# Linear attention and a gated causal convolution on one core: tokens of q in sequence, every load on GpSimd's queue, and new tables of order

## The chip, the core and the metric

The kernel runs on one NeuronCore of one Trainium2 chip. The core has five engines with instruction streams of their own: PE (TensorE, matrix products and transposes), DVE (VectorE), ACT (ScalarE), POOL (GpSimd) and SP (SyncE, which here only issues transfers). They meet through semaphores. Sixteen DMA engines move data between the chip's memory and the core's SBUF. [...] PE writes to PSUM, eight banks of 128 partitions by 2 KB.

The metric is the device time of one execution in microseconds, the median of several runs. Lower is better. The kernel before took 217.03 us (three runs, 216.33 to 217.27).

## The reference

The inputs q, k, v have the shape (batch 8, heads 8, tokens 576, 64), float32. The features have 128 + 128 columns.

```python
def phi(x):
    proj = np.einsum('bhsd,df->bhsf', x, w_phi)
    proj = proj - np.max(np.abs(proj), axis=-1, keepdims=True)
    return np.concatenate([np.exp(proj), np.exp(-proj)], axis=-1)
q_p, k_p = (phi(q), phi(k))
kv = np.einsum('bhsf,bhsd->bhfd', k_p, v)
z = np.sum(k_p, axis=2)
num = np.einsum('bhsf,bhfd->bhsd', q_p, kv)
den = np.einsum('bhsf,bhf->bhs', q_p, z)[..., None] + 1e-06
x = num / den                        # then (b, s, heads * 64)
gate_pre = sum over k of conv_w[k] * x shifted by 4 - k tokens     # causal, 5 taps
gate = 1.0 / (1.0 + np.exp(-gate_pre))
out = gate * (x @ w_val) @ w_out     # (8, 576, 512) float32
```

## The kernel before

**The stages of one batch.** The eight batches run through the same stages, several batches in flight. A batch has 36 groups of 128 rows of k and as many of q; they are worked in five units, `UNITS` (four of 4 columns of 128, one of 2).

- *Load and transpose.* k and q are brought to SBUF with rows on the partitions and must be transposed to `kT` and `qT` (the 64 features of a row on the partitions, two rows side by side). Batch 0 is loaded as float32 by SP (`load32`, L521 to 527), transposed by PE in float32 (`tp32`, L536) and copied to bfloat16 by ACT or DVE (`tc32`, L542 and L544). Batch 1 is loaded as bfloat16 by POOL (`load`, L550) and transposed by PE (`tp16`, L555, copied at L560). From batch 2 on POOL loads to `KQN` and SP issues one DMA transpose for k and one for q (`xpose`, L565). Two small POOL copies (`hold`, `holdx`, L509 and L512) hold POOL's next loads back until earlier data have landed. v comes from SP (`loadv`, L531) but for batch 1.
- *The k side.* `kp` (PE, L577) projects; `kmax` (DVE, L585) takes maxima of the absolute values; `kexp` (ACT, L595) makes e^x and e^-x to `KTIL`; `ek` (ACT, L604) makes the scale of each row; `vs` (POOL, L610 and L611) scales v to `VT`; `st` (PE, L620) sums over tokens to the 65 columns of kv and z; `kv` copies them to bfloat16.
- *The q side.* `qm` and `qmax` (L577, L585), `mqt` and `mqr` (L658 to 670, the maxima transposed and negated), `rx` (POOL, L682: the maxima spread over an identity, so that a product with ones subtracts them), `qp` (PE, L693 and L698), `qexp` (ACT, L706 to `QTIL`, and for the last unit L709 to `QTT`).
- *Quotient and transpose back.* `num` (PE, L719, five chunks; the fifth is L726), `nrm` (DVE, L737 the reciprocal, L740 the product), `xtp` (PE, L748 and L752, or for batches 6 and 7 a DMA transpose by SP, `xtd`, L755) and `xtc`, which copies to `XT`, x with its 512 columns on the partitions. `halo` (POOL, L768 and L769) fills the tokens to the left of each half.
- *The MLP.* `gate` (PE, L781, the convolution as products with diagonal matrices), `tanh` (ACT, L785; the sigmoid is made from it), `val` (PE, L791), `gv` (DVE, L797), `gvc` (POOL, L805, collects the last 64 tokens of two batches), `out` (PE, L813 and L817), `oev` (the copy from PSUM, L630 or L634) and `odma` (the store by SP, 256 KB in rows of 2 KB, L830 and L836).

**Order of the tokens.** q of a batch is loaded as 128 equal contiguous rows of 9 KB (`rows`, L518), 16 partitions to a head. So a column of `qT` holds tokens 36 apart, the chunks of `num` hold every second row pair, and a chunk is not a stretch of the sequence: `XT` has two halves of 144 pairs of tokens, and `halo` copies what the causal shift needs from one place of this order to another. `num` of any chunk waits for all of `qexp` of its batch.

**Order of the work.** Nothing is scheduled on the chip or at build time. `build` lists about a thousand tasks; `ORDER` gives the order in which they are issued (each engine takes its own in that order), `FLEX` which of two or three engines takes a task that can go to several, and `BANKS` the PSUM banks. `WARM` puts in products of ones (6 here, L491), `ZERO` adds products with zeros to a PSUM bank in use (150 here, L497 and L504) at places in the first quarter of the order. An engine waits at an instruction until its data are there, and all behind it on that engine wait too.

Of the kernel before, what the change touches and what calls it, by code (L numbers as in the profile page):

```python
# [17 lines left out]
F = 128  # L18
DM = 512
# [5 lines left out]
NU = len(UNITS)  # L25
PEB = 1
QPART = ((0, 1), (2, 3, 4))
XB = (6, 7)
HOLDU = 4
NO = 8  # L30
NJ = 2 * NC
XH = R // 2
HALO = 16
XW = HALO + XH
WARM = (
    "60:6:1 81:1:1 87:7:2 134:7:1 141:7:1 "
)
ZERO = "35:76:7 61:80:5 75:34:1 101:105:1 126:215:8 144:223:1 155:192:4 158:200:1 175:315:6 189:346:1 195:241:2 197:241:2 211:327:1"
STD = 1.18
E1 = D + 1  # L40
QW = 2 * NR

ORDER = (
# [36 lines left out]
)  # L80
FLEX = (
    "AAAAAADAAADDPPPPDDDDAADDDDDDDDDDDDDAAADAAAADDDDAAADDDAADAAADDADAADDDDADDDDADDDDDDAADADDAAAAAA"
)
BANKS = (
    "037362307001454523232323016701676714232367230101676012354423010145454501013660564675601456745010145450101676767014501454"
    "545672012376701230167676745677773567232367232345452301672323232367674545015452343623670101232345454452230145450167676767"
    "010123014501230167450120167364012345236745454555723014545234567232323010123236745230167232346701422010167454567010121656"
    "701456701012301670123010167232367674567023677260123230123230167464644501016701670123676745672345232345450123670157672345"
    "010167452326322345670145670101674545012345012367452345010127452301014545670101765"
# [3 lines left out]
class Task:  # L93

    __slots__ = ("kind", "b", "u", "engs", "durs", "fn", "deps", "grp", "also", "opens", "mode", "eng", "lat", "idx", "wait", "rank")
# [5 lines left out]


def out_seq(b, c):
    return 9 * (b // 2) + (4 * (b % 2) + c)


LAT = {"PE": 0.17, "ACT": 0.17, "DVE": 0.17, "POOL": 0.2, "SP": 0.7, "DMA": 1.3}
MSW = 0.05


def dve(n, ov=0.075):
    return n / 960.0 + ov


def act(n):
    return n * 0.000833 + 0.067


class Plan:
# [9 lines left out]
    def add(self, kind, b, u, eng, dur, fn=None, deps=(), grp=None, mode=0, lat=None, also=None, wait=0.0, rank=None):  # L129
        t = Task()  # L130
        t.kind, t.b, t.u, t.fn = kind, b, u, fn
        t.engs = (eng,) if isinstance(eng, str) else eng
        t.durs = (dur,) if isinstance(eng, str) else dur
        t.deps = [d for d in deps if d is not None]
        t.grp, t.also, t.mode, t.lat, t.wait, t.rank = grp, also, mode, lat, wait, rank
        t.opens = []
        for g in (grp, also):
            if g is not None:
                if g.left == 0:
                    t.opens.append(g)  # L140
                g.left += 1
        t.eng = t.engs[0]
        t.idx = len(self.tasks)
        self.tasks.append(t)
        return t

    def follow(self):

        names = {"A": "ACT", "D": "DVE", "P": "POOL"}
# [13 lines left out]
def build(plan, em=None):  # L163
# [11 lines left out]
    def G(*k):  # L175
        return h.get(k)
# [724 lines left out]
```

## Time and profile before

One profiled execution has a span of 215.4 us from the first to the last instruction; the runs' median of 217.03 us includes the start and end around it.

| | us | share of the span |
|---|---|---|
| span of the profiled execution | 215.4 | |
| median of the runs | 217.03 | |
| ACT: `kexp` and `qexp` (L595, L706, L709) | 71.8 + 62.5 + 10.0 | 67% |
| ACT: all | 180.6 | 84% |
| DVE: the two maxima (L585) | 44.3 + 43.6 | 41% |
| POOL: all, of it `vs` (L610) | 132.9, 67.9 | 62%, 32% |
| mean busy share of the 16 DMA engines, the queue of SP and ACT | | 56.8% |
| the same, POOL's queue | | 26.2% |

A row of a group reads: line, engine, operation, output tile and input tile with their shapes, count, then the busy time of all and the mean of one in ns, then the idle time ahead of them and who ended it. The mean of one is longer than busy time over count where instructions overlap. In a view of stretches each engine has its busy time and, in brackets, its instructions; PEclk is the clock that the throttle granted (1.00 is full). In a timeline a row reads start, duration, engine, line, what, and how many are merged. "SPq" and "POOLq" rows of DMA issues are the issue; the time to landing stands in the view of transfers.

### The profile page before, as it was taken

The numbers are of one execution on the slowest core, as the hardware profiler recorded it, in microseconds if no ns is written. First come the engines' busy times: TensorE is split into PE (matmuls) and PEld (weight loads), VectorE is DVE, ScalarE is ACT, GpSimd is POOL, SyncE is SP. The second block draws the span as 40 slices with busy tenths as digits, with TensorE's granted clock in tenths as the row PEclk, the third lists the DMA queues.
The fourth block names the chain that finished last, engine by engine and source line by source line (L and its number), as shares of the span: only waits on it lengthen the run. The fifth ranks groups of instructions, "written<-read, shape, count | busy, mean of one in ns | idle before, by whom it ended". The sixth has DMA issues, their size and how long they took to land.

```text
span 215.4 us, 9005 instructions
## 1 busy us (share of the span) xinstructions
PE 194.6 (90%) x3924; PEld 138.9 (64%) x3944; DVE 170.2 (79%) x257; ACT 180.6 (84%) x267; POOL 132.9 (62%) x172
## 2 busy tenths in 40 slices
PE   2887978778999999989999999999999999899990
PEld 2665566566766767667767677568757766687640
DVE  3299999999699978998899978998699897654510
ACT  3699999999999899998899997999988988634251
POOL 3045999996984649952997099903992879210010
PEclk9999999999999999999999999999999999999998
DMA  6999979999799699979997878979962264864166
GB/s 180 381 226 208 291 162 159 277 198 199 139 165 286 118 153 250 290 130 200 237 279 134 96 165 251 188 151 173 287 211 84 67 161 126 83 168 99 49 188 205
DMA packets 49954, 39.92 MB, mean 185 GB/s; under 512 B 34165, under 2 KB 39541, under 8 KB 49914
## 3 DMA queue, kind: packets, MB, share of 16 engines
q1 hardware_dynamic: 43616, 28.65, 56.8%
q0 software_dynamic: 6032, 10.49, 26.2%
q8 instruction: 31, 0.51, 1.0%
q10 hardware_dynamic: 266, 0.21, 0.3%
q14 instruction: 9, 0.07, 0.1%
HBM read 30.48 MB, written 9.44 MB: 185 GB/s over the span
## 4 chain that ended last, share of the span: by engine, by line
PE 55%; ACT 18%; DVE 15%; issue 4%; DMA 4%; SPq 0%; DVEq 0%; ACTq 0%
PE PS L791 12%; PE PS L781 9%; PE PS L813 9%; ACT QTIL L706 7%; ACT KTIL L595 7%; DVE MQP L585 6%; PE PS L719 5%; PE PS L577 5%; PE PS L620 4%; DVE MK L585 2%; PE PS L693 2%; DMA KTIL<-in_k_dram 2%; DMA XT<-XN 2%; PE PS L536 2%; DVE XN L740 2%
## 5 line engine op out<-in xcount | busy, mean ns | idle before, releaser
L595 ACT ACTIVATE KTIL<-PS 128x1024 bf16<-128x1024 f32 (+1 forms) x80 | 71.8, 965 | 3.5 <-PE PS L577 1.7
L610 POOL TENSOR_TENSOR VT<-VN,EK 128x1152 bf16<-128x1152 f32 x32 | 67.9, 2123 | 2.9 <-ACT EK L604 2.8
L706 ACT ACTIVATE QTIL<-PS 128x1024 bf16<-128x1024 f32 x64 | 62.5, 1051 | 1.9 <-PE PS L698 1.4
L682 POOL TENSOR_TENSOR RX<-MQR,ident 128x512 bf16<-128x512 bf16 (+1 forms) x39 | 36.6, 963 | 36.2 <-DVE MQR L670 32.8
L585 DVE TENSOR_REDUCE MK<-PS 128x8 f32<-128x1024 f32 (+1 forms) x40 | 44.3, 1113 | 2.9 <-PE PS L577 1.2
L585 DVE TENSOR_REDUCE MQP<-PS 128x8 bf16<-128x1024 f32 (+1 forms) x40 | 43.6, 1112 | 2.1 <-PE PS L577 1.2
L791 PE MATMUL PS<-XT,WV 128*128 128x288 bf16 x256 | 34.8, 286 | 0.3 <-DVE GV L797 0.2
L797 DVE SCALAR_TENSOR_TENSOR GV<-TH,PS 128x576 bf16<-128x576 bf16 x32 | 23.8, 752 | 10.4 <-PE PS L791 4.7
L813 PE MATMUL PS<-WOUT,GV 128*128 128x512 bf16 x110 | 29.7, 380 | 1.1 <-issue 0.2
L791 PEld LDWEIGHTS <-WV 128*128 128x128 bf16 x256 | 23.8, 98 | 7.9 <-issue 1.4
L785 ACT ACTIVATE TH<-PS 128x576 bf16<-128x576 f32 x32 | 20.4, 663 | 9.3 <-PE PS L781 5.9
L781 PE MATMUL PS<-XT,GW 64*64 64x288 bf16 x640 | 23.2, 285 | 0.8 <-DMA XT<-XN 0.7
L620 PE MATMUL PS<-VT,KTIL 64*128 64x65 bf16 x1152 | 23.1, 191 | 0.7 <-issue 0.6
L740 DVE TENSOR_TENSOR XN<-PS,RCP 128x512 bf16<-128x512 f32 x32 | 22.1, 692 | 1.4 <-DMA XT<-XN 0.3
L620 PEld LDWEIGHTS <-KTIL 64*128 64x128 bf16 x1152 | 20.7, 95 | 3.3 <-issue 2.3
L719 PEld LDWEIGHTS <-QTIL 128*128 128x128 bf16 x512 | 18.3, 97 | 6.4 <-issue 4.1
L719 PE MATMUL PS<-KV,QTIL 128*128 128x65 bf16 x512 | 20.3, 193 | 0.4 <-DVE MQP L585 0.2
L781 PEld LDWEIGHTS <-GW 64*64 64x64 bf16 x640 | 17.8, 106 | 3.4 <-issue 0.8
L634 ACT ACTIVATE OUTS<-PS 128x512 f32<-128x512 f32 x22 | 13.5, 619 | 7.3 <-PE PS L813 6.1
L813 PEld LDWEIGHTS <-GV 128*128 128x128 bf16 x128 | 11.1, 98 | 11.3 <-issue 0.6
L577 PE MATMUL PS<-W,qT 64*128 64x128 bf16 x288 | 15.2, 219 | 2.7 <-ACT QTIL L706 1.0
L577 PEld LDWEIGHTS <-qT 64*128 64x128 bf16 x288 | 10.7, 95 | 9.1 <-issue 4.3
(79 smaller groups left out, 235.0 us busy)
## 6 DMA issues: line engine op xcount, KB each, us to landing
out_dram<-OUTS SPq DMA_DIRECT2D x32, 256.0 KB, 3.4
VN<-in_v_dram SPq DMA_DIRECT2D x7, 1152.0 KB, 6.4
KQN<-in_q_dram POOLq DMA_DIRECT2D x6, 576.0 KB, 8.3
KQN<-in_k_dram POOLq DMA_DIRECT2D x6, 576.0 KB, 9.6
KTIL<-in_k_dram SPq DMA_DIRECT2D x4, 288.0 KB, 4.3
VN<-in_v_dram POOLq DMA_DIRECT2D x1, 1152.0 KB, 11.5
KTIL<-in_q_dram SPq DMA_DIRECT2D x4, 256.0 KB, 5.0
out_dram<-OUTS SPq DMA_DIRECT2D x14, 64.0 KB, 2.4
```

The costliest lines, as they stand in the source:

```text
L577: nc.tensor.matmul(self.PS[:, t.grp.banks[par], i * P:(i + 1) * P], X[rows, (c0 + i) * P:(c0 + i + 1) * P], self.W2[rows, :], start=True, ...
L585: self.nc.vector.tensor_reduce(o, self.two(t.grp, n * P).rearrange("p a (c f) -> p a c f", f=F), AX.X, ALU.max, apply_absolute_value=True)
L595: self.nc.scalar.activation(self.KTIL[b % 2][:, s, c0:c0 + n, :, :].rearrange("p c a f -> p a c f"), self.two(t.grp, n * P).rearrange("p a ...
L610: nc.gpsimd.tensor_tensor(self.VT[g][:, s, :, 0:D], self.VN[b % 2][:, NC * g:NC * g + NC, :], e.to_broadcast([P, NC, D]), ALU.mult)
L620: nc.tensor.matmul(self.PS[:, t.grp.banks[ab], (s * 2 + x) * E1:(s * 2 + x + 1) * E1], self.KTIL[b % 2][rows, s, J // 2, J % 2, :], self.V ...
L682: self.nc.gpsimd.tensor_tensor(o, *wide(self.MQR[self.mq(b, u)][:, :], self.ident2), ALU.mult)
L706: self.nc.scalar.activation(o, i, AF.Exp, scale=1.0 - 2.0 * s)
L719: nc.tensor.matmul(self.PS[:, t.grp.banks[h // 4], (h % 4) * E1:(h % 4 + 1) * E1], Q[:, s, c % 2, h, (c // 2) * P:(c // 2 + 1) * P], self. ...
L740: nc.vector.tensor_tensor(o.rearrange("p (g h) d -> p g h d", g=ng), n[:, :, :, 0:D], rc.unsqueeze(3).to_broadcast([P, ng, 4, D]), ALU.mult)
L781: self.nc.tensor.matmul(self.PS[o * D:(o + 1) * D, t.grp.banks[par], 0:R], self.GW[r, jj, 4 - m, :], X[r, 4 * a + jj, :, HALO - 8 * s:HALO ...
L791: self.nc.tensor.matmul(self.PS[:, t.grp.banks[par], 0:R], self.WV[:, i, (2 * j + par) * D:(2 * j + par + 2) * D], X[:, 4 * par + i, :, HA ...
L813: nc.tensor.matmul(self.PS[:, t.grp.banks[0], :], GV[:, j, c % 2, (c // 2) * XH:(c // 2) * XH + P], self.WOUT[:, j, c % 2, :], start=(j == ...
```

## The change

**q in sequence.** q of every batch is loaded in five pieces of 128 tokens (the last of 64) of all heads, 16 partitions to a head and 8 (4) neighbouring tokens to a partition, each piece a DMA of its own:

```diff
+KLOAD = (((0, 1), (1, 1), (2, 2)), ((0, 4),))
+QLOAD = ((tuple((i, 1) for i in range(5)),) * 2)
...
+    def load(self, t, w, b, p0, n):
...
+        x = self.src["q"][b]
+        c0 = 4 * p0
+        if p0 < 4:
+            self.nc.gpsimd.dma_start(N[:, c0:c0 + 4, :].rearrange("p y c -> p (y c)"), x[:, p0 * P:(p0 + 1) * P, :].rearrange("h (i t) d -> h i (t d)", i=16))
         else:
...
+            self.nc.gpsimd.dma_start(N[:, 16:18, :].rearrange("p y c -> p (y c)"), x[:, 4 * P:S, :].rearrange("h (i t) d -> h i (t d)", i=16))
```

With that a unit of q is a chunk of `num`, so `num` of a chunk waits for `qexp` of that chunk alone; `QTT` is gone, and the last unit is one ACT instruction of 512 columns instead of two of 256. The order inside a chunk is put right when x is transposed back, by a permuted identity as the moving operand (`perm`, two of them, made by DVE at the start). `XT` then holds the 288 pairs of a batch in sequence, `halo` and `gvc` are gone, and the DMA transposes `xtd` of batches 6 and 7 are replaced by PE's:

```diff
+        o = self.QTIL[b % 2][:, s, :, u * P:u * P + n * 32].rearrange("p h (a r) -> p a h r", a=2)
+        self.nc.scalar.activation(o, self.two(t.grp, n * P).rearrange("p a (h r) -> p a h r", h=H), AF.Exp, scale=1.0 - 2.0 * s)
...
+            o = ps.rearrange("p (a j u r) -> p u j a r", a=2, j=4, u=2)
+            for u in range(2):
+                for j in range(4):
+                    nc.tensor.transpose(o[:, u, j], self.XN[i][:, u, j * P:(j + 1) * P], self.perm[0][:, :])
...
-    def halo(self, t, b):
-        X = self.XT[b % 2][:, :, :, :].rearrange("p h k (y x) -> p (h k) y x", x=8)
-        self.nc.gpsimd.tensor_copy(X[:, :, 0:2, 1:8], X[:, :, 18:20, 0:7])
-        self.nc.gpsimd.tensor_copy(X[:, 1::2, 0:2, 0:1], X[:, 0::2, 18:20, 7:8])
```

**All loads on POOL.** k, q and v of all batches and both large weights are issued by POOL. k of batch 0 comes in three pieces; batch 0 is bfloat16 on arrival and goes through the bfloat16 transposes of PE, as batch 1 does. `hold` and `holdx` are gone; a load into `KQN` waits itself for the DMA transpose that reads the buffer. The copy of 64 columns of `WV` is a POOL copy instead of a DMA. In the built program the loads of POOL take eight semaphores in turn, and a load's issue waits until the load that used its semaphore eight loads earlier has landed. Ahead of POOL's first `rx` stand 22 loads: k of batch 0 (3), a piece of q0, k of batch 1, then q1, q0, q0, q0, q0, q1, q1, v of batch 0, `WV`, q2, q1, k of batch 2, q1 and four more of q2. w_phi and conv_w are loaded by SP.

**The first and the last MLP in two column parts.** For batches 0 and 7 `gate`, `tanh`, `val` and `gv` are made for pairs 0 to 127 and 128 to 287 apart:

```diff
+COLS = {b: ((0, R),) for b in range(B)}
+COLS[0] = ((0, P), (P, R))
+COLS[B - 1] = ((0, P), (P, R))
...
+        for z, (x0, x1) in enumerate(COLS[b]):
+            xs = [h["xtc", b, i] for i in range(3) if i * P < x1 and min(R, (i + 1) * P) > x0 - (1 if x0 else 0)]
```

**Stores.** Two chunks of 128 pairs of tokens become one buffer [128, 2, 512] and one store of 512 KB in rows of 4 KB (`store`); the last chunk of batch 7 goes as two halves by SP and ACT (`store1`). The last 32 pairs of two batches are made by products with 32 columns each (`out4`, 64 of them instead of 32 with 64 columns).

```diff
+    def store(self, t, b, kk):
+        d = self.out_d[b][2 * P * kk:2 * P * (kk + 1), :].rearrange("(r a) o -> r (a o)", a=2)
+        self.nc.sync.dma_start(d, self.OUTS[(2 * b + kk) % NO][:, :, :].rearrange("p a o -> p (a o)"))
```

**Tables.** `ORDER`, `FLEX`, `BANKS` and `WARM` are new; `ZERO` is gone, with its 150 products of zeros, and `WARM` has 9 products, at three places in the start. The reciprocal is a task of its own (`rcp`), `mqr` may go to ACT, and `vs` of batch 0 may go to DVE, which takes one of the four. What the new `FLEX` moves, by instructions in the whole program: copies of kv, DVE 12 to 7 and ACT 4 to 9; of `OUTS`, DVE 14 to 17 and ACT 22 to 19 (both with the four of the last pairs); of `XT` in the large size, DVE 10 to 15 and ACT 2 to 1; the copies of `kT` and `qT`, DVE 7 to 10 and ACT 9 to 4.

More of the change, by code (lines that the diff above doesn't have):

```diff
@@ L90 @@
 )
 class Task:
-    __slots__ = ("kind", "b", "u", "engs", "durs", "fn", "deps", "grp", "also", "opens", "mode", "eng", "lat", "idx", "wait", "rank")
+    __slots__ = ("kind", "b", "u", "engs", "fn", "deps", "grp", "opens", "mode", "eng", "idx", "n")
 class Group:
     __slots__ = ("kind", "nb", "left", "banks", "idx")
[L103 to L112, printed above, removed]
@@ L115, in act @@
-def act(n):
-    return n * 0.000833 + 0.067
 class Plan:
@@ L147, in follow @@
     def follow(self):
-        names = {"A": "ACT", "D": "DVE", "P": "POOL"}
+        names = {"A": "ACT", "D": "DVE", "P": "POOL", "S": "SP"}
         for t, f in zip([t for t in self.tasks if len(t.engs) > 1], FLEX):
@@ L160, in parts, with pieces @@
     return QPART if b == 0 else (tuple(range(NU)),)
+def pieces(b):
+    return ((0, 8), (8, 8), (16, 2)) if b else ((0, 4), (4, 4), (8, 8), (16, 2))
+VE = ("DVE", "ACT")
 def build(plan, em=None):
@@ new lines, in build @@
+            h["idf"] = A("idf", 0, 0, "POOL", fn("c_idf"))
+            h["id"] = A("idb", 0, 0, "DVE", fn("c_idb"), [h["idf"]])
+            h["idc"] = A("idc", 0, 0, "DVE", fn("c_idc"), [h["idf"]])
+            x = A("lw", b, 0, "SP", fn("c_w"))
+            x = A("DMA", b, 0, "DMA", None, [x], n="lw")
+            h["w"] = A("wc", b, 0, "DVE", fn("c_w2"), [x])
+            x = A("lcw", b, 0, "SP", fn("c_cv"))
+            h["lcw"] = A("DMA", b, 0, "DMA", None, [x], n="lcw")
+        land = {"k": [], "q": []}
@@ L256, in build @@
-        ld = h["lv0",] = A("lv", b, 0, "POOL" if b == 1 else "SP", 0.65, fn("loadv", b),
-               [G("vs", b - 2, g, s) for g in range(2) for s in range(2)] + [G("lv0",) if b > 2 else None],
-               rank=-980 if b == 0 else None)
-        h["lv", b] = A("lv", b, 0, "DMA", 3.6, None, [ld])
+        if True:
+            x = A("lv", b, 0, "POOL", fn("loadv", b), [G("vs", b - 2, g, s) for g in range(2) for s in range(2)])
+            h["lv", b] = A("DMA", b, 0, "DMA", None, [x], n="lv")
@@ new lines, in build @@
+        if b == 0:
+            x = A("wv", b, 0, "POOL", fn("c_wv"), [])
+            x = A("DMA", b, 0, "DMA", None, [x], n="wv")
+            h["wv"] = A("wvx", b, 0, "POOL", fn("c_wvx"), [x])
+            x = A("wo", b, 0, "POOL", fn("c_wo"), [])
+            h["wo"] = x = A("DMA", b, 0, "DMA", None, [x], n="wv")
+            x = A("wod", b, 0, "SP", fn("c_dupo"), [x])
+            h["wod"] = A("DMA", b, 0, "DMA", None, [x], n="wod")
+            g = plan.group("cw", 1)
+            x = A("cw", b, 0, "PE", fn("c_cw"), [h["lcw"], h["idf"]], g, 0)
+            x = A("cw2", b, 0, "DVE", fn("c_cw2"), [x], g)
+            h["gw"] = [A("cgt", b, i, "POOL", fn("c_gt", i), [x, h["idc"]]) for i in range(2)]
@@ L276, in build @@
         for gi in range(2):
             for s in range(2):
-                h["vs", b, gi, s] = A("vs", b, gi, "POOL", 2.22, fn("vs", b, gi, s),
-                                      [eks[gi % len(eks)], G("lv", b)] + [G("st", b - 1, gi, x) for x in range(2)])
+                h["vs", b, gi, s] = A("vs", b, gi, ("POOL", "DVE") if b in VSD else "POOL", fn("vs", b, gi, s),
+                                      [h["ek", b, gi], h["lv", b]] + [G("st", b - 1, gi, x) for x in range(2)])
             g = plan.group("st", 2)
@@ L286, in build @@
                 sts.append(st)
[L287 to L288 removed]
+            h["kv", b, gi] = A("kv", b, gi, VE, fn("kv", b, gi), sts + [G("num", b - 2, c) for c in range(5)], g)
         for u, (c0, n) in enumerate(UNITS):
             g = plan.group("qm", 2)
[L293 removed]
@@ L321, in build @@
+            rc = A("rcp", b, c, "DVE", fn("rcp", b, c), [num, G("nrm", b - 1, c)], g)
+            h["nrm", b, c] = A("nrm" if c < 4 else "nrm4", b, c, "DVE", fn("nrm", b, c), [rc, G("xtp", b - 1, c // 2)], g)
             if c in (1, 3, 4):
                 i = c // 2
-                nrms = [G("nrm", b, cc) for cc in ((0, 1), (2, 3), (4,))[i]]
-                war = [G("gate", b - 2, j) for j in range(4)] + [G("val", b - 2, j) for j in range(4)]
-                if i < 2 and b in XB:
-                    xt = h["xtp", b, i] = A("xtp", b, i, "SP", 1.4, fn("xtd", b, i), nrms + war, lat=-0.2)
-                    h["xtc", b, i] = A("xtc", b, i, "DMA", 1.45, None, [xt])
-                    h["xtp", b, i] = h["xtc", b, i]
-                    continue
@@ L330, in build @@
-                g = plan.group("xtp", 1)
-                xt = h["xtp", b, i] = A("xtp", b, i, "PE", 0.54 if i < 2 else 0.22, fn("xtp", b, i), nrms, g, 0)
-                h["xtc", b, i] = A("xtc", b, i, ("DVE", "ACT"), (dve(512), act(1024)) if i < 2 else (dve(256), act(256)), fn("xtc", b, i), [xt] + war, g)
-        halo = A("xtc", b, 3, "POOL", 0.6, fn("halo", b), [G("xtc", b, 2)] + [G("gate", b - 2, j) for j in range(4)])
-        xall = [G("xtc", b, i) for i in range(3)] + [halo]
-        for j in range(4):
-            g = plan.group("gate", 2)
-            gt = h["gate", b, j] = A("gate", b, j, "PE", 0.62, fn("gate", b, j), xall, g, 3)
-            h["tanh", b, j] = A("tanh", b, j, "ACT", act(576), fn("tanh", b, j), [gt, G("gv", b - 1, j)], g)
@@ new lines, in gvs @@
+        def gvs(b, x0, x1):
+            return [h["gv", b, j, z] for j in range(4) for z, (y0, y1) in enumerate(COLS[b]) if y0 < x1 and y1 > x0]
+        for kk in range(2):
+            oes = []
+            war = stores[-NO] if len(stores) >= NO else None
+            for a in range(2):
+                g = plan.group("out", 1)
+                o = h["out", b, 2 * kk + a] = A("out", b, a, "PE", fn("out", b, a, kk), gvs(b, kk * P, kk * P + P) + [h["wod" if a else "wo"]], g, 0)
+                oes.append(A("oev", b, a, VE, fn("oev", b, a, 2 * b + kk), [o, war], g))
+                if b == B - 1 and kk == 1:
+                    x = A("st1", b, a, ("SP", "ACT"), fn("store1", b, kk, a), [oes[a]])
+                    x = A("DMA", b, a, "DMA", None, [x], n="st1")
+            if not (b == B - 1 and kk == 1):
+                x = A("st2", b, kk, "SP", fn("store", b, kk), oes)
+                x = A("DMA", b, kk, "DMA", None, [x], n="st2")
+                stores.append(x)
@@ new lines, in build @@
+        if b % 2:
+            g = plan.group("out4", 1)
+            o = A("out4", b, 4, "PE", fn("out4", b), gvs(b, 2 * P, R) + gvs(b - 1, 2 * P, R) + [h["wod"]], g, 4)
+            h["out", b, 4] = h["out", b - 1, 4] = o
+            oe = A("oev", b, 4, VE, fn("oev4", b), [o, G("st4", b // 2 - 2, 0), G("st4", b // 2 - 2, 1)], g)
+            for a in range(2):
+                x = A("st4", b, a, ("SP", "ACT") if b == B - 1 else "SP", fn("store4", b, a), [oe])
+                h["st4", b // 2, a] = A("DMA", b, a, "DMA", None, [x], n="st4")
@@ L365 @@
+    return plan
+EKS = (0,)
+VSD = (0,)
 class Emit:
```

516 lines of the change are left out of this document (182 added, 334 removed), and 75 rows, old and new, of the table ORDER.

## The prediction, made before the changed kernel ran

> **What bounds the kernel now.** I read the page's head, then the stretches, then the timeline of the first 22 us, the chain of waits at the end, and the groups of POOL.
>
> ```profile
> span 215.4 us, 9005 instructions
> ...
> 0.00:21.24 21.24, 14.66 (x174) 10.77 (x175) 12.85 (x18) 14.73 (x24) 7.55 (x20) 1.00 0.94 249
> 8.68:21.24 12.56, 10.58 (x146) 7.74 (x147) 11.00 (x12) 11.68 (x20) 5.69 (x8) 1.00 1.06 246
> 21.24:177.40 156.16, 147.83 (x3189) 105.83 (x3201) 140.19 (x208) 147.61 (x216) 117.00 (x139) 1.00 0.90 190
> 177.40:215.40 38.00, 32.12 (x569) 22.26 (x568) 17.20 (x33) 18.23 (x29) 8.38 (x14) 0.97 0.56 132
> 21.50:50.00 28.50, 23.51 (x600) 18.00 (x602) 26.93 (x43) 28.15 (x38) 27.61 (x28) 1.00 1.04 215
> 150.00:175.00 25.00, 24.84 (x466) 17.25 (x466) 21.58 (x31) 21.72 (x34) 19.02 (x24) 1.00 0.56 163
> ```
>
> The columns are the stretch, its length, then the busy time of PE, PE's weight loads, DVE, ACT and POOL. There are three parts. Up to 21.24 us (the first `qexp`) the pipeline fills. Up to 177.4 us (the first `qp` of batch 7) ACT sets the pace: busy 147.61 of 156.16, 94.5%, and DVE 140.19. PE drops behind with the MLP meanwhile: early it has time (23.51 of 28.5), late none (24.84 of 25), and there ACT falls to 21.72 of 25. From 177.4 us only PE matters: 32.12 us of work, and ACT half idle.
>
> ```profile
> 5.58 0.23 DVE L455 CAST W<-W 128x128 bf16<-128x128 f32 x1 [2.92 <-DMA W<-in_w_phi_dram]
> ...
> 7.60 1.03 PE L577 MATMUL PS<-W,kT 64*128 64x128 bf16 x16
> ...
> 8.68 1.94 ACT L595 ACTIVATE KTIL<-PS 128x1024 bf16<-128x1024 f32 x2 [0.39 <-PE PS L577]
> ...
> 12.69 0.76 POOL L550 DMA_DIRECT2D KQN<-in_k_dram  x1
> ...
> 12.85 0.39 PE L577 MATMUL PS<-W,qT 64*128 64x128 bf16 x8
> ...
> 16.83 2.04 POOL L682 TENSOR_TENSOR RX<-MQR,ident 128x512 bf16<-128x512 bf16 x2 [3.38 <-DVE MQR L667]
> ```
>
> The first `kexp` runs at 8.68 us, after w_phi is there (5.58) and k has gone through PE.
>
> **The fill.** In the changed kernel k of batch 0 is transposed as bfloat16, but DVE makes W2, the identity and the permutations first, and w_phi still has to land. The first `kexp` can come at 7 us (w_phi 2 us earlier, bfloat16 copies) or at 9.2 (w_phi as late as now, and some 2 us of small DVE work and a copy behind it); I take 8.0. The order then gives ACT, ahead of the first `qexp`:
>
> ```profile
> L595 ACT ACTIVATE KTIL<-PS 128x1024 bf16<-128x1024 f32 x64 | 63.4, 1055 | 2.1 <-DVE MK L585 0.9 <-DVE GV L797 0.5 <-PE PS L577 0.4
> ...
> L595 ACT ACTIVATE KTIL<-PS 128x512 bf16<-128x512 f32 x16 | 8.8, 602 | 1.5 <-PE PS L577 1.3
> ...
> L740 DVE TENSOR_TENSOR XN<-PS,RCP 128x512 bf16<-128x512 f32 x32 | 22.1, 692 | 1.4 <-DMA XT<-XN 0.3
> ...
> L632 ACT COPY XT<-PS 128x1024 bf16<-128x1024 bf16 x2 | 2.1, 1049 | 0.0
> ```
>
> 11 large exponentials (3 of batch 1) by 63.4/64 are 10.9, 2 small by 8.8/16 are 1.1, two large bfloat16 copies 2.1, and `ek`, `mqr` and a small copy 1.2 by like rows: 15.3 us. At 93%, ACT's density from 8.68 to 21.24 now (11.68 of 12.56), they end at 24.5. That is later than 21.24, with three exponentials of batch 1 already done.
>
> Does the data keep up? POOL issues 22 loads before its first `rx`, and the 22nd waits until the 14th (WV) has landed. Up to WV that is 6.56 MB of source: k and q of batch 0, k and three fifths of q of batch 1, v, WV. Now seven tensors of 1.18 MB (k0, q0, v0, and k and q of batches 1 and 2) have landed by 22.3, the last load's issue at 12.69 plus its median landing.
>
> ```profile
> KQN<-in_k_dram POOLq DMA_DIRECT2D x6, 576.0 KB, 9.6
> ...
> VN<-in_v_dram SPq DMA_DIRECT2D x7, 1152.0 KB, 6.4
> ...
> VN<-in_v_dram POOLq DMA_DIRECT2D x1, 1152.0 KB, 11.5
> ```
>
> That is 8.26 MB in 21.6 us, 383 GB/s of source, so WV is there at about 18 us, and after the last issue `rx` starts at 18.5 to 21 instead of 16.83; one `rx` (1.04) and `qp` put `qexp` at 20.3 to 23, still inside ACT's 24.5. The cover is thin: a load path a fifth slower would show on ACT. Bounds for the first `qexp`: 21.3 and 28.
>
> **The middle.** What ACT does in all changes little: nine copies of float32 `kT` and `qT` gone 4.9, four bfloat16 ones added 2.8, five copies of kv +3.3, three of `OUTS` -1.8, `XT` -0.7, one exponential of 512 for two of 256 -1.2, three `mqr` +0.6, `tanh` in halves +1.0: 180.6 becomes 179.6. Less 17.0 before the first `qexp` (15.3, a copy and the table load) and 17.9 from the first `qp` of batch 7 on (now 18.23), 144.7 lie between. At today's 94.5% that is 153.1, so the first `qp` of batch 7 comes at 177.6. `qexp` writes runs of 64 instead of 32 elements and `gate` reads at odd offsets; no row shows either, and I take no cost. DVE gains some 4 us in all (one `vs`, copies moved), under ACT's line. PE loses the slow float32 transposes and gains 32 of x (0.45 for eight, below); both lie where PE has time or beside ACT.
>
> **The tail.** From the first `qp` of batch 7 PE is now busy to the end at 210.47.
>
> ```profile
> 122.09 0.86 PE PS L813 x4
> ...
> 149.34 0.98 PE PS L719 x32
> ...
> 155.91 0.45 PE PS L748 x8
> ...
> 183.74 4.44 DMA XT<-XN
> ...
> 209.47 1.00 PE PS L817 x8
> ...
> 210.54 0.60 ACT OUTS L634
> ```
>
> The new order leaves less work behind that point. Gone from it: five `out` of batches 4 and 5 (five times 0.86), one `out` of the last pairs (1.00), and `num` of batch 6 (four times 0.49 and 0.37 for the fifth), with 0.1 of small things: 7.7. Come in: two `xtp` of batch 7 (0.90) in place of DMA transposes, and 0.3 for matrices of half width. So 33.1 (177.40 to 210.47) less 6.5 is 26.6. The 4.44 us in which the chain waited for a DMA transpose was covered by `num` and `out` on PE, and I give nothing for it. `num` of a chunk no longer waits for all of `qexp`, but at the end reciprocal, product (0.69 by L740's row above), transpose (0.45) and copy still follow one another, covered by four `val` and three `out` of batch 6; I take 2.0 of stalls (0 to 4). The last pairs' 16 products with 32 columns take 1.00 as the 8 with 64 do if four run side by side, 2.0 if two do; I take the first, and the second is inside the stalls' bound. The end behind PE (a copy, the last store) stays 4.9: that store is of 256 KB in both kernels. The other stores, two a batch instead of four, are issued by SP, which has nothing else but DMA transposes now and no loads; they lie under PE's and ACT's work, and where a store came late its `oev` would wait, for which four buffers of 512 KB are held, as much as eight of 256 now.
>
> Sum: 24.5 + 153.1 + 26.6 + 2.0 + 4.9 = 211.1 against the span of 215.4, 4.3 less; on the runs' 217.03 that is **212.7 us**. Its own range is 209 to 216.
>
> **The rivals.**
>
> *POOL becomes the bound (219.5 us; chance 0.28).*
>
> ```profile
> L610 POOL TENSOR_TENSOR VT<-VN,EK 128x1152 bf16<-128x1152 f32 x32 | 67.9, 2123 | 2.9 <-ACT EK L604 2.8
> ...
> L550 POOL DMA_DIRECT2D KQN<-in_q_dram x6 | 3.5, 589 | 0.5 <-issue 0.5
> ...
> L805 POOL COPY GVT<-GV 128x128 bf16<-128x128 bf16 x16 | 4.4, 323 | 11.0 <-DVE GV L797 11.0
> ...
> L768 POOL COPY XT<-XT 128x224 bf16<-128x224 bf16 x8 | 3.0, 374 | 12.9 <-DVE XT L628 6.7 <-ACT XT L632 6.2
> ...
> L531 POOL DMA_DIRECT2D VN<-in_v_dram x1 | 0.8, 813 | 0.0
> ...
> POOL RX L682 <- DVE MQR L670: 32.8, 6, 8.9
> ```
>
> Of 156.16 us in the middle POOL works 117.0 and idles 39.2. Gone are `halo`, `gvc` and `hold`, 8.7 there; added are 20 issues of q by 0.589 (11.8), 7 of v by 0.813 (5.7), and some 1.6 of copies and moved `rx`: 127.4 in 153.1, 25.7 idle. Its waits are long because it runs ahead: 32.8 on `mqr`, 6.7 on `XT`, which goes. If the 32.8 stay (32.5 of the idle), the middle takes 6.8 more, 219.5. The point from which it decides is 25.7 us of waiting. For it speaks that `rx` and `vs` now stand behind loads that wait for DMA transposes, and that the one v load on POOL landed after 11.5 us, against 6.4; v of batch 5 is issued behind v of batch 6 and only a few us ahead of its `vs`. Against it, those waits are slack, which shrinks first. [...]
>
> *The array stays slow in the fill (218.1; 0.15).* Sixteen products took 1.03 at 7.60 us, 64 ns each, but eight took 0.39 at 12.85, 49 ns.
>
> ```profile
> L504 PE MATMUL PS<-ONES,NIL 64*128 64x128 bf16 x140 | 5.6, 216 | 0.0
> ```
>
> Those fillers, 150 up to 42 us, are gone. If PE's own work up to there (17.5 us of the 23.5 and what lies before) runs at 64 instead of 49 and all of it shows, it costs 5.4. ACT has other work for most of it, so I think little shows. [...]
>
> *The middle gets denser (206.1; 0.15).* From 21.5 to 50 us ACT runs at 28.15 of 28.5, 98.8%; with PE's backlog gone it might so throughout: 144.7/0.988 is 146.5, 6.6 less. Against it, DVE is as full as ACT.
>
> **How the numbers follow.** The forecast has 0.42, POOL 0.28, the slow array 0.15, the denser middle 0.15. Half a per cent, 215.95 to 218.1, is about what a measurement can tell from no change. Faster: 0.34 of the forecast's, all 0.15 of the denser middle, 0.03 of the others: 0.52. Same: 0.05, 0.03 and 0.04: 0.12. Slower: 0.03, 0.24 and 0.09: 0.36. The range runs from 206.5, near the denser middle, to 220.5, a little past POOL's.
>
> **What would show it.** Right: first `kexp` near 8 us, first `qexp` near 24.5; ACT at 94 to 95% until the first `qp` of batch 7 near 178; PE done some 28 us later; no wait for a DMA transpose in the chain's last 40 us. Wrong: ACT waiting for `qp` and these for `rx` or `vs`, POOL above 85% in the middle (its rival); `L577`'s successors at 64 ns after 15 us (the slow array); a first `rx` after 23 us, with ACT idle before it, would mean that the loads are slower than 383 GB/s.

## The result, and the profile after

The changed kernel took 478.12 us (median of 4 runs, 473.61 to 479.12), the kernel before 217.15 beside it (4 runs): 2.19 times as long, 95% interval 2.179 to 2.210. 212.7 was predicted, and 220.5 was the end of the range. Runs of one and the same kernel further down differ by up to 3.6% (e9, 241.45 to 250.21 us), so where two kernels lie near each other their lowest runs are compared too.

The head of the page of the changed kernel, and its stretches of 100 us (columns as in the prediction: PE, weight loads, DVE, ACT, POOL, clock, DMA share, GB/s):

```profile
span 475.9 us, 9222 instructions
...
PE 288.2 (61%) x4085; PEld 188.3 (40%) x4085; DVE 178.9 (38%) x275; ACT 188.7 (40%) x259; POOL 150.6 (32%) x171
...
PEclk9999999556586655955767655565997967799897
```

```profile
0.00:100.00 100.00, 55.11 (x743) 39.22 (x744) 45.11 (x70) 40.87 (x60) 49.84 (x64) 0.93 0.63 118
100.00:200.00 100.00, 58.58 (x815) 38.68 (x816) 34.16 (x54) 40.40 (x52) 25.50 (x29) 0.65 0.35 65
200.00:300.00 100.00, 61.66 (x804) 38.56 (x801) 32.85 (x44) 37.95 (x51) 30.69 (x33) 0.61 0.45 95
300.00:400.00 100.00, 64.61 (x941) 40.21 (x938) 43.07 (x61) 43.70 (x60) 35.48 (x36) 0.74 0.26 60
400.00:475.90 75.90, 48.22 (x792) 31.66 (x790) 23.71 (x47) 25.82 (x38) 9.03 (x9) 0.88 0.14 50
```

No stage stands out and no engine is the bound: ACT, 94% busy in the middle before, is busy 34 to 44% in every stretch. The work grew little (ACT 188.7 us of 180.6, DVE 178.9 of 170.2). The 80 exponentials of k, now and before (busy time, mean of one in ns, idle time ahead of them):

```profile
L531 ACT ACTIVATE KTIL<-PS 128x1024 bf16<-128x1024 f32 (+1 forms) x80 | 72.9, 939 | 85.7 <-DVE XN L660 18.7
```

```profile
L595 ACT ACTIVATE KTIL<-PS 128x1024 bf16<-128x1024 f32 (+1 forms) x80 | 71.8, 965 | 3.5 <-PE PS L577 1.7
```

So the instructions are as long as before, and each waits. PE's 288 us are the same products that take 193.4 in e1 below, at a lower clock: 0.93 in the first stretch, 0.61 to 0.88 in the others. The waits of this kernel (engine and line that waited, who released it, us in all, times, longest):

```profile
POOL RX L607 <- DVE MQR L485: 114.1, 5, 48.2
...
DVE GV L708 <- ACT QTIL L629: 24.6, 9, 5.4
DVE MQP L521 <- ACT QTIL L629: 23.4, 7, 8.2
...
ACT KTIL L531 <- DVE XN L660: 18.7, 8, 4.7
...
ACT QTIL L629 <- PE PS L702: 14.9, 5, 5.1
```

In the first the need is real, as `rx` reads `mqr`. The others are pairs that have nothing to give each other. `gv` does not read what `qexp` makes; `kexp` does not read `nrm`'s product; `qexp` needs nothing of `val` (L702). What they share is PSUM. The first such wait comes early, in the timeline (start, duration, engine, line, what; in brackets the idle time and who ended it):

```profile
7.81 0.61 PE L513 MATMUL PS<-W,kT 64*128 64x128 bf16 x8
...
8.35 1.67 PE L494 MATMUL PS<-ident,KTIL 128*128 128x128 bf16 x14
...
10.06 1.22 DVE L521 TENSOR_REDUCE MK<-PS 128x8 f32<-128x1024 f32 x1 [2.04 <-PE PS L494]
...
11.32 1.02 ACT L531 ACTIVATE KTIL<-PS 128x1024 bf16<-128x1024 f32 x1 [1.74 <-DVE MK L521]
```

The first `kmax` reads the eight products that ended at 8.42 us. `BANKS` has put them into banks 0 and 2. It starts at 10.06, when the transposes at L494 end; eight of those 14 write bank 1. Instructions on a pair of banks address it by a stepped slice, `self.PS[:, a:b + 1:b - a, ...]` (`two`): its two ends are the banks a and b, and it waits as if it read bank 1 as well. Then `kexp` waits for `kmax`, a reader of the same two banks, though both only read.

In the kernel before all 239 groups of two banks have neighbours, so nothing lies between. In the changed kernel 74 of 255 have; 65 are three banks apart (two lie between), 45 four, 39 five or more, 32 two.

### The profile page after: what moved, and what is told of

Same layout as the page of the kernel before. It is cut to its first block, busy times and chain, and to the rows that moved or that the text cites. A ratio compares the mean times of both kernels' runs of the same rounds, so it can differ in the third digit from the quotient of the medians.

```text
span 475.9 us, 9222 instructions
## 1 busy us (share of the span) xinstructions
PE 288.2 (61%) x4085; PEld 188.3 (40%) x4085; DVE 178.9 (38%) x275; ACT 188.7 (40%) x259; POOL 150.6 (32%) x171
## 5 line engine op out<-in xcount | busy, mean ns | idle before, releaser
L629 ACT ACTIVATE QTIL<-PS 128x1024 bf16<-128x1024 f32 (+1 forms) x80 | 72.7, 938 | 91.1 <-PE PS L702 14.9
L521 DVE TENSOR_REDUCE MQP<-PS 128x8 bf16<-128x1024 f32 (+1 forms) x40 | 44.5, 1117 | 73.4 <-ACT QTIL L629 23.4
L702 PE MATMUL PS<-XT,WV 128*128 128x288 bf16 (+2 forms) x320 | 53.1, 332 | 20.7 <-ACT QTIL L629 6.1
L714 PE MATMUL PS<-WOUT,GV 128*128 128x512 bf16 x128 | 44.7, 496 | 7.4 <-DVE MQP L521 2.4
L702 PEld LDWEIGHTS <-WV 128*128 128x128 bf16 x320 | 34.0, 121 | 37.1 <-issue 27.1
L692 PE MATMUL PS<-XT,GW 64*64 64x288 bf16 (+2 forms) x800 | 36.8, 323 | 16.9 <-ACT TH L696 6.7
L708 DVE SCALAR_TENSOR_TENSOR GV<-TH,PS 128x576 bf16<-128x576 bf16 (+2 forms) x40 | 24.8, 632 | 58.1 <-ACT QTIL L629 24.6
L639 PE MATMUL PS<-KV,QTIL 128*128 128x65 bf16 x512 | 28.7, 226 | 23.3 <-ACT QTIL L629 6.9
L696 ACT ACTIVATE TH<-PS 128x576 bf16<-128x576 f32 (+2 forms) x40 | 21.4, 555 | 49.7 <-PE PS L692 18.6
L618 PE MATMUL PS<-qT,W 64*128 64x512 bf16 (+1 forms) x80 | 22.0, 477 | 25.9 <-ACT KTIL L531 10.3
L513 PE MATMUL PS<-W,kT 64*128 64x128 bf16 x288 | 21.0, 276 | 18.0 <-ACT KTIL L531 6.5
L513 PEld LDWEIGHTS <-qT 64*128 64x128 bf16 x288 | 14.7, 119 | 31.1 <-issue 30.0
```

The costliest lines, as they stand in the source:

```text
L513: nc.tensor.matmul(self.PS[:, t.grp.banks[par], i * P:(i + 1) * P], X[rows, (c0 + i) * P:(c0 + i + 1) * P], self.W2[rows, :], start=True, ...
L521: self.nc.vector.tensor_reduce(o, self.two(t.grp, n * P).rearrange("p a (c f) -> p a c f", f=F), AX.X, ALU.max, apply_absolute_value=True)
L629: self.nc.scalar.activation(o, self.two(t.grp, n * P).rearrange("p a (h r) -> p a h r", h=H), AF.Exp, scale=1.0 - 2.0 * s)
L639: nc.tensor.matmul(self.PS[:, t.grp.banks[h // 4], (h % 4) * E1:(h % 4 + 1) * E1], Q[:, s, h, c * P:(c + 1) * P], self.kvh(b, s, h), start ...
L692: self.nc.tensor.matmul(self.PS[o * D:(o + 1) * D, t.grp.banks[par], 0:x1 - x0], self.GW[r, jj, 4 - m, :], X[r, 4 * a + jj, HALO - s + x0: ...
L702: self.nc.tensor.matmul(self.PS[:, t.grp.banks[par], 0:x1 - x0], self.WV[:, i, (2 * j + par) * D:(2 * j + par + 2) * D], X[:, 4 * par + i, ...
```

## The experiments

Theory (banks): an instruction on two banks waits, and is waited for, over all banks between them. Rivals: POOL's loads, each of which waits for one eight loads earlier; the new order in itself; the array's clock, as a cause and not a result, since the fillers are gone.

**e1, neighbouring banks.** Only `BANKS` is new, made for the changed kernel's own order so that every pair is (i, i + 1); `WARM`'s banks follow.

```diff
 WARM = (
-    "16:7:5 49:7:1 58:5:3 "
+    "16:0:5 49:7:1 58:0:3 "
...
 BANKS = (
-    "031434151020316274517560345172403445656231704561710404700140714145607562356072323141407140777625212035623235607231717170"
+    "023041311564523670123014501230145016767456701236750101544010101012367012323676745232367450657210030456767452301236723232"
...
```

> The changed kernel with one table new: BANKS, in which every group of two banks has neighbours (in the changed kernel 74 of 255 have), with the banks of WARM's fillers to match. ORDER, FLEX, loads, transposes and stores as in the changed kernel. Theory (banks): an instruction that reads two banks by a stepped slice waits, and is waited for, as if it touched every bank between them; with neighbours nothing lies between, so the time falls from 478 to 208 to 225 us, each engine's busy time stays, and the mean granted clock goes back above 0.95. Rival (loads on POOL's queue) and rival (the new order is bad in itself): over 400 us, nothing of theirs is touched. Rival (the slow clock is the cause, since the fillers are gone): over 400 us at a clock near 0.75, as the fillers are still gone.

Measured: 244.64 us (240.8 to 246.84), 1.128 times before (1.118 to 1.137), clock 0.944 in the profiled execution, a little under the 0.95 that was expected. The same `kmax` now starts 0.05 us behind its products:

```profile
7.64 0.61 PE L513 MATMUL PS<-W,kT 64*128 64x128 bf16 x8
...
8.30 1.23 DVE L521 TENSOR_REDUCE MK<-PS 128x8 f32<-128x1024 f32 x1 [0.44 <-PE PS L513]
```

A table of banks is worth 233 us, and the clock comes back with no filler added: all three rivals fall as the main cause. But 208 to 225 was expected; the rest is taken up from e5 on.

**e2, the changed kernel's banks, one instruction for each.** Its own `BANKS`, order and loads; only what an instruction touches is made exact.

```diff
-    def two(self, g, n, c=0):
+    def two(self, g, n):
         a, b = g.banks
-        return self.PS[:, a:b + 1:b - a, c:c + n]
+        if b - a == 1:
+            return [(slice(0, 2), self.PS[:, a:b + 1, 0:n])]
+        return [(slice(i, i + 1), self.PS[:, x:x + 1, 0:n]) for i, x in enumerate(g.banks)]
...
```

Each place that uses `two` then runs its instruction once for every part of this list.

> The changed kernel with its own BANKS, ORDER and loads; each instruction that reads two banks that are no neighbours is made two, one for each bank. Theory (banks): the waits for the banks between go, so it falls below 260 us; the price is 142 more instructions on ACT and 143 more on DVE, at 0.149 us (twice 602 ns less 1055) and 0.155 us (twice 687 less 1219): 21 and 22 us more work, so 230 to 250 us. Rivals (loads, order, clock): more work and nothing taken away, 478 to 500 us.

Measured: 241.44 us (240.24 and 242.64), as expected, with 285 more instructions on ACT and DVE than the changed kernel and half its time. Their price was less than reckoned: ACT has 185.6 us of work and DVE 186.2, 6.5 and 7.1 more than in e1, not 21 and 22. So it is not which bank a group has, it is the span of the access.

**e3 and e4, the kernel before with its banks renamed.** Nothing else is touched.

```diff
-            g.banks = [int(x) for x in BANKS[i:i + g.nb]]
+            g.banks = [[0, 4, 1, 5, 2, 6, 3, 7][int(x)] for x in BANKS[i:i + g.nb]]
...
-                warm[int(i)] = (int(bank), int(n))
+                warm[int(i)] = ([0, 4, 1, 5, 2, 6, 3, 7][int(bank)], int(n))
```

(e4 has 0, 1, 2, 4, 3, 5, 6, 7 in its place.)

> The kernel before with its banks renamed and nothing else: 0 to 7 become 0, 4, 1, 5, 2, 6, 3, 7, so that each of its 239 pairs has three banks between. Theory (banks): the same loss without any of the rest of the change, 400 to 600 us, clock below 0.85. Rivals (loads, order, clock): a name of a bank changes nothing, 217 us.

> The kernel before with banks 3 and 4 swapped and nothing else: the pairs of 113 of its 239 groups, (2,3) and (4,5), become (2,4) and (3,5), with one bank of the other between; the other 126 stay neighbours. Theory (banks): a part of the loss, 260 to 360 us. Rivals (loads, order, clock): 217 us.

Measured: e3 659.16 us, e4 318.14 us, one run each. Heads of the two pages, e3 first:

```profile
span 657.4 us, 8997 instructions
...
PE 348.8 (53%) x3923; PEld 218.2 (33%) x3944; DVE 177.2 (27%) x257; ACT 192.4 (29%) x267; POOL 133.3 (20%) x172
```

```profile
span 316.4 us, 8983 instructions
...
PE 224.7 (71%) x3924; PEld 156.2 (49%) x3944; DVE 172.9 (55%) x257; ACT 184.7 (58%) x267; POOL 132.6 (42%) x172
```

The kernel before, with no part of the change in it, loses 100 us where 113 pairs have one bank between and 441 where all have three; e3 was beyond what was expected. The look is the changed kernel's: busy time of DVE, ACT and POOL within 7% of before, all idle by turns, and PE dear by its clock (mean 0.563 in e3). The cause is shown from both sides.

That a stepped slice counts for the banks it skips is what e1 to e4 show; that readers wait for readers rests on rows such as `kexp`'s above, 1.74 us idle until `kmax` had ended.

**e5, e6, e7, e8: what is left.** Each is e1 with one part more. e5 gives DVE's product `vs` back to POOL (one letter of `FLEX`), e6 loads v from batch 2 on by SP, e7 makes the last two stores of 128 KB four of 64 KB, e8 is all three.

```diff
-    "DDDADDDAPPADPAAPPDPPPDDADDAADADDADDDDDDDADADADADDDAAADAAAADDDDADDAADDDDDDADDAADDDDAAADDADADDAADDADDDDAADAAAASDSA"
+    "DDDADDDAPPAPPAAPPDPPPDDADDAADADDADDDDDDDADADADADDDAAADAAAADDDDADDAADDDDDDADDAADDDDAAADDADADDAADDADDDDAADAAAASDSA"
...
-        eng = self.nc.gpsimd if t.eng == "POOL" else self.nc.sync
+        eng = self.nc.gpsimd if b < 2 else self.nc.sync
...
+        for i in range(2):
+            p0 = a * D + i * 32
+            eng.dma_start(d[i], self.OUT4[b // 2 % 2][p0:p0 + 32, :])
```

> The changed kernel with neighbouring banks (e1) and one letter of FLEX new: the product vs of batch 0 that the change moved to DVE goes back to POOL. In e1 it takes 7.13 us on DVE while POOL works without a pause, 1.40 us in the changed kernel; the copy of q behind it is then 6.3 us late for PE, and qexp 5.8 late for ACT. Theory (DVE and POOL shut each other out): DVE loses 9.1 us there (7.13 and 1.96 for its cast), POOL gains 2.4, so 4 to 7 us less than e1's 244.6: 237 to 241 us. Rival (the loads set the fill): the copy waits for something else, 243 to 247 us.

> The changed kernel with neighbouring banks (e1); v of batches 2 to 7 is loaded from SP's queue, as before the change, instead of POOL's. Theory (POOL's queue of loads is what is left): POOL is free of 6 issues of 0.83 us, and its 5.7 us of waits for v go, so 3 to 8 us less than e1: 237 to 242 us. Rival (the loads are late because their buffers are): v waits on SP behind stores and transposes instead, 243 to 250 us.

> The changed kernel with neighbouring banks (e1); the two last stores of 128 KB (64 rows) are made four of 64 KB, as before the change. In e1 9.3 us lie between PE's last product and the end, 4.9 before the change, and after the first 4 us one or two of 16 DMA engines are busy. Theory (long stores at the end): 2 to 4 us less than e1: 240.5 to 242.5 us. Rival (the 512 KB store is what trails): 244 to 245 us.

> e5, e6 and e7 in one. Theory (the three are separate terms): the gains add, 225 to 236 us. Rival (one wait behind all): the gain of the best of them alone.

Measured: e5 250.24 us (246.89 to 250.87), e6 247.58 (245.4 to 250.46), e7 237.91 (237.31 to 238.61), e8 245.92 (244.88 to 247.46), against e1's 244.64 (240.8 to 246.84). Only e7 gains: 6.7 us by the medians, 3.5 by the lowest runs, where 2 to 4 was expected. e6 went as its rival had it. e8 missed both of its expectations: it lies 8.0 above e7, so the gains do not add, and the best of them is lost. In e1 the last copy ends at 230.38 and the span at 239.0:

```profile
229.78 0.60 ACT L489 ACTIVATE OUTS<-PS 128x512 f32<-128x512 f32 x1 [1.13 <-PE PS L714]
230.40 0.33 SPq L733 DMA_DIRECT2D out_dram<-OUTS  x1
```

That is 8.6 us; in e7 it is 231.87 to 235.7, 3.8. The 4.8 us between them is all that this edit touches. It halves each of the two stores and also takes its outermost dimension, two batches, out of it; which of the two counts was not tested.

e5 is a miss that teaches. Its first part came true: the first `tanh` stands at 45.63 us instead of 52.49. But then ACT stands still for 12.09 us, where e1 has no such gap: POOL's next load waits 14.7 us for the DMA transpose of q of batch 2. The gain, and more, is given back at the next wait.

**e9 and e10: loads beside DMA transposes.** e9 is e5 and e7 together. e10 issues v of batch 1 and w_out earlier, in a time when the DMA engines move nothing (0 GB/s from 32.5 to 38.75 us in e9):

```diff
-206 79 80 211 103 109 102 243 101 207 81 116 244 108 110 117 208 249 250 43 330 118 111 51 241 247 82 112 45 242
+206 79 208 45 80 211 103 109 102 243 101 207 81 116 244 108 110 117 249 250 43 330 118 111 51 241 247 82 112 242
```

This is a part of `ORDER`; 208 is v of batch 1, 45 is w_out, 80 the third `vs`.

> e5 and e7 in one: neighbouring banks, the product vs back on POOL, short last stores. Both theories below are measured against it; by the medians so far 250.2 less e7's gain of 6.7: 242 to 246 us.

> e9, with two loads moved in ORDER: v of batch 1 and w_out are issued ahead of the third vs of batch 0, some 7 to 9 us earlier. In e5 they and v of batch 2 are issued at 37.3, 39.3 and 41.7 us, while q of batch 2 is transposed by the DMA engines (issue at 38.76, 8.74 us long, 3.38 in e1), and w_out lands after 15.0 us (5.7 in e1); POOL's next load waits 14.7 us for that transpose, and ACT idles 12.1 us. From 32 to 38 us the DMA engines move nothing. Theory (loads and DMA transposes hold each other up): the wait of 14.7 falls below 7, ACT's gap of 12.1 below 6, and the time by 5 to 12 us against e9. Rival (the transpose is late by its buffers alone): wait and gap stay above 11 and the time within 3 us of e9.

Measured: e9 246.74 us (241.45 to 250.21), just above its 242 to 246, e10 241.14 (238.45 to 243.84). SP's issue of the transpose and POOL's next load, e9 and then e10:

```profile
39.91 10.26 SPq L500 DMA_TRANSPOSE qT<-KQN  x1
...
56.95 0.66 POOL L475 DMA_DIRECT2D KQN<-in_q_dram  x1 [12.01 <-DMA qT<-KQN]
```

```profile
41.92 2.78 SPq L501 DMA_TRANSPOSE qT<-KQN  x1
...
54.17 0.66 POOL L476 DMA_DIRECT2D KQN<-in_q_dram  x1 [6.92 <-DMA qT<-KQN]
```

The issue falls from 10.26 to 2.78 us, the wait from 12.01 to 6.92 and ACT's gap from 9.05 to 4.04, as the theory has it. But the load behind the wait stands only 2.8 us earlier (54.17 against 56.95); the rest of the shorter wait is POOL coming to it later. The medians differ by 5.6 us, the lowest runs by 3.0, so a gain of 5 to 12 us is not shown.

**e11, the fillers.** The kernel before with `ZERO = ""`.

> The kernel before without its 150 zero products into open groups (ZERO empty); nothing that is computed changes. Rival of the prediction (the array stays slow in the fill without fillers): up to 5.4 us more, 219 to 223 us, and products of 8 at 0.5 us or more after 15 us. Theory (little of it shows, ACT has other work): 216 to 219 us.

Measured: 219.67 us, 1.006 times before (1.002 to 1.011). The first two stretches:

```profile
0.00:26.00 26.00, 19.89 (x171) 13.13 (x172) 16.90 (x26) 18.76 (x31) 12.51 (x25) 0.80 0.99 256
26.00:50.00 24.00, 18.34 (x439) 13.24 (x438) 22.37 (x32) 23.15 (x30) 22.65 (x24) 0.86 1.00 194
```

The clock does fall without them (0.80 and 0.86, 1.00 before), and it costs 1.4 us, not 5.4: ACT has 23.15 of 24 us of work all the same. (219.67 lies at the near end of the range that the expectation gave to the rival.)

**e12, no loads of v.** e7 with `loadv` empty from batch 2 on; the products use the v of batches 0 and 1 again.

```diff
     def loadv(self, t, b):
+        if b >= 2:
+            return
```

> e7 (neighbouring banks, short last stores) with the loads of v of batches 2 to 7 left out, 7.1 MB of source; the products use the v of batches 0 and 1 again. Everything else is computed. Theory (what is left between 100 and 150 us, ACT busy 37.79 of 50 in e7 against 46.88 before the change, is loads and DMA transposes holding each other up): ACT's 37.79 rises above 42 there, and the time falls from 237.9 to 222 to 232 us. Rival (transposes wait for their own q and k, in five pieces): under 40 there, 234 to 239 us.

Measured: 234.97 us (232.19 to 236.08), ACT busy 38.34 of the 50 us in the profiled execution, both as the rival had it. Nearly a quarter of all source bytes gone moves little: for v's loads, the theory of loads against transposes does not hold in this stretch. A few us there are chance: e1 and e7, alike up to their last stores, have ACT at 41.12 and 37.79.

**e13, a gap for DVE.** e7 with e10's two loads moved, the product still on DVE.

> e7 with the loads of v of batch 1 and of w_out moved ahead in ORDER as in e10, the product vs still on DVE. POOL then issues two loads, some 1.6 us, just when DVE's product begins, and computes nothing meanwhile. Theory (DVE and POOL shut each other out while one of them computes): the product takes 1.4 to 3 us, not 7.13 as in e1; with e10's gain 226 to 235 us against e7's 237.9. Rival (a product of this form is slow on DVE beside any POOL work, or the 7.13 came from elsewhere): over 5 us, 234 to 239 us.

Measured: 238.89 us (236.44 to 240.32). The product first in e1, with what POOL does meanwhile:

```profile
30.24 7.13 DVE L547 TENSOR_TENSOR VT<-VN,EK 128x1152 bf16<-128x1152 f32 x1
30.29 0.25 POOL L548 CAST VT<-EK 128x18 bf16<-128x18 f32 x1
30.44 2.60 POOL L607 TENSOR_TENSOR RX<-MQR,ident 128x256 bf16<-128x256 bf16 x3
...
33.01 2.11 POOL L547 TENSOR_TENSOR VT<-VN,EK 128x1152 bf16<-128x1152 f32 x1
...
35.20 0.86 POOL L464 DMA_DIRECT2D VN<-in_v_dram  x1
```

and in e13:

```profile
29.92 1.77 DVE L548 TENSOR_TENSOR VT<-VN,EK 128x1152 bf16<-128x1152 f32 x1
31.61 7.75 DVE L549 CAST VT<-EK 128x18 bf16<-128x18 f32 x1
```

```profile
30.06 0.86 POOL L465 DMA_DIRECT2D VN<-in_v_dram  x1
30.92 0.77 POOL L430 DMA_DIRECT2D WOUT<-in_moe_w_out_dram  x1
31.70 2.61 POOL L608 TENSOR_TENSOR RX<-MQR,ident 128x256 bf16<-128x256 bf16 x3
...
39.25 0.81 POOL L465 DMA_DIRECT2D VN<-in_v_dram  x1
```

The product takes 1.77 us while POOL only issues loads. But the cast behind it, 18 elements a partition, then takes 7.75: it begins as POOL starts to compute and ends at 39.36, just after POOL turns to its next load. In e1 the product ends at 37.37; with some 1.4 us of its own (its length in the changed kernel) it was let in near 36, in POOL's load of 35.20 to 36.06. The wait has moved by one instruction, and DVE is free at the same time as in e1; so for these two instructions the theory is borne out, and the gain in time (226 to 235 us was expected) did not come. In the changed kernel the product took 1.40 us, begun at 45.14 us among POOL's three `rx`, and there these took 3.72 us (2.60 in e1). Not every instruction of DVE is held up: a copy from PSUM took 0.68 us beside POOL's `vs` (29.64 us in e1). In e1 and e13 DVE stood behind several of POOL's instructions in a row; 7.13 us against 1.77 speaks against giving DVE that product, and the prediction counted it as work alone.

## Why the prediction was wrong, point by point

**The step that failed is the tables.** The prediction took `BANKS` as a name for where things lie and costed it at nothing. It asked of every wait that the change adds on queues, loads and stores, and not of those on PSUM. It never looked at which banks a pair has, nor at how `two` addresses them. That left out 233 of the 265 us by which it was wrong (e1 against the changed kernel), and no rival had it.

**The rest, by its own terms,** can be checked in e7, where the bank waits are gone. Its stretch from the first `qexp` to the first `qp` of batch 7:

```profile
25.64:201.35 175.71, 151.43 (x3253) 110.31 (x3265) 145.69 (x211) 145.69 (x207) 130.27 (x139) 0.91 0.80 167
```

- *Work.* ACT was to have 144.7 us of work in the middle; it has 145.69. POOL was to have 127.4; it has 130.27. The counting of instructions held.
- *The middle's density.* 94.5% was carried over from before; it is 145.69 of 175.71, 82.9%, and the middle takes 22.6 us more than the predicted 153.1. This is the term that remains once the banks are right. Most of it lies in two holes. e7 and then before:

```profile
26.00:50.00 24.00, 13.58 (x281) 10.56 (x281) 19.16 (x20) 12.57 (x16) 16.16 (x17) 0.60 0.87 191
...
100.00:150.00 50.00, 41.87 (x848) 29.30 (x846) 34.97 (x50) 37.79 (x56) 31.68 (x35) 0.90 0.93 198
```

```profile
26.00:50.00 24.00, 19.36 (x544) 15.28 (x546) 22.79 (x35) 23.72 (x31) 23.11 (x24) 1.00 1.02 205
...
100.00:150.00 50.00, 49.25 (x1030) 34.91 (x1032) 45.08 (x70) 46.88 (x71) 33.45 (x44) 1.00 0.90 183
```

  ACT does 11.2 us less in the first and 9.1 less in the second. In the first it stands still for 3.68 us at a copy of kv, which waits through `st` for POOL's `vs`; POOL came to its work only at 23.99 us, behind its loads. Then it stands still for 5.82 us, because DVE's product takes so long beside POOL (7.13 us in e1, alike up to the last stores), and when that is taken away (e5) the transposes of q of batch 2 stand in its place (12.09 us). Of the second it is shown that v's loads are not its main cause (e12). The chain of waits of e7 has a DMA transpose of q of batch 5 in it, 9.68 us long. SP issued it when the last of the five pieces of that q had landed. POOL's timeline and then the chain, both of e7:

```profile
118.65 1.04 POOL L607 TENSOR_TENSOR RX<-MQR,ident 128x512 bf16<-128x512 bf16 x1 [7.35 <-DVE MQR L485]
119.63 0.64 POOL L475 DMA_DIRECT2D KQN<-in_q_dram  x1
```

```profile
123.64 9.68 DMA qT<-KQN
```

  The second row is that last piece. In POOL's order it stands behind an `rx` for which POOL waited 7.35 us. Why `mqr` was late stays open, and no run moved that load.
- *The fill.* First `kexp` 8.0 predicted (7 to 9.2), 9.7 in e7: the new order has `kmax` ahead of it on the same two banks, from 8.42 to 9.64 us, and before the change `kexp` went first. First `qexp` 24.5 predicted, 25.75 there, inside its bounds. But the loads were mis-sized.

```profile
23.40 0.58 POOL L475 DMA_DIRECT2D KQN<-in_q_dram  x1 [2.65 <-DMA WV<-in_moe_w_val_dram]
23.99 2.04 POOL L607 TENSOR_TENSOR RX<-MQR,ident 128x512 bf16<-128x512 bf16 x2
...
25.75 1.94 ACT L629 ACTIVATE QTIL<-PS 128x1024 bf16<-128x1024 f32 x2 [0.42 <-PE PS L623]
```

  WV has landed at 23.4 instead of 18, and the first `rx` stands at 23.99 instead of 18.5 to 21: 6.56 MB in 22.7 us, 289 GB/s where 383 was taken. That is past the condition the prediction named (a load path a fifth slower), and the first `rx` stands after the 23 us that it gave as a sign of slow loads. At the first `qexp` it shows by 0.42 us alone, because ACT's own work there ended no earlier than 25.33; so it is luck that the slow loads moved that point so little. They show behind it, in the 3.68 us above. Why they are slower stays open. The rows quoted for 383 had k, whose type is changed on the way, at 9.6 us and v on SP's queue, unchanged, at 6.4; but in e6 the median is 6.8 us for k on POOL's queue and 8.6 for v on SP's, so a change of type alone does not explain it.
- *The tail.* 28.6 us were predicted from the first `qp` of batch 7 to PE's last product (26.6 and 2.0 of stalls); e7 has 29.9 (201.35 to 231.23). That is near, but by two misses that offset each other: PE works 29.41 us there where 26.6 had been counted, and stands still for 0.47 where 2.0 had been taken.
- *The end* "stays 4.9: that store is of 256 KB in both kernels". Wrong: the last store to be issued is one of 512 KB, and the end took 9.3 in e1. Not that store trails, though, but the two of 64 rows by 2 KB: with these cut in half the end is 4.5 (e7).
- *The rivals.* The slow array was real and worth 1.4 us in the kernel before (e11, clock 0.80 up to 26 us against 1.00). POOL as the bound did not come over the middle as a whole, at 130.27 of 175.71 us (74%), but what spoke for it did: work on POOL stood behind loads that wait for DMA transposes (e9, 12.01 us). And in the last 44 us of the middle, 158.18 to 202.00, e7's chain of waits runs over POOL's `vs`, `rx` and loads alone:

```profile
158.18 2.14 POOL VT L547
...
185.23 6.30 DMA VN<-in_v_dram
...
198.16 2.08 POOL VT L547
```

  There it cost little, as ACT is still busy 45.84 of 50 us from 150 to 200. That v lands later on POOL's queue did not come true: its median is 7.8 us there in e7 and 8.6 on SP's in e6. The denser middle was the wrong way round.

No version here beats the kernel before; the best of the changed kernel's family by its median is e7 at 237.9 (e12, lower, leaves loads out).

## What to carry to other kernels

Before a table of buffers or banks is taken as free, look at how the code addresses them: here a slice with a step was guarded over its whole span, and pairs of banks that were not neighbours tied together the engines that used a bank between (659.16 us in e3 against 217.85). The sign of it in these profiles was that all engines idled by turns, with their work nearly unchanged (ACT 188.7 us of 180.6), waiting for engines whose results they don't read (`gv` for `qexp`, 24.6 us). When a density is carried over to a changed order, ask which wait would end last if one of its covers went; e5 and e13 each removed a wait and found the next one at the same place.

## What the runs showed that was not expected

- A renaming of banks alone made a tuned kernel 3.0 times as slow (e3, 659.16 against 217.85 us).
- DVE's product took 7.13 us behind POOL's instructions (e1), 1.77 beside two of POOL's load issues (e13) and 1.40 in the changed kernel; a cast of 18 elements a partition took 7.75 (e13).
- PE's mean clock was lower, the more the whole kernel waited: 0.995, 0.899, 0.755 and 0.563 at spans of 215.4, 316.4, 475.9 and 657.4 us, and its products took longer with it (348.8 us in e3 for 194.6 before). From stretch to stretch of the changed kernel it does not follow how busy PE is: 0.93 with PE busy 55.11 of 100 us, 0.61 with 61.66.
- Two last stores of 64 rows of 2 KB kept the end waiting 8.6 us behind the last copy; as four of 32 rows, 3.8.
